# Moving the small tiles of a memory-attention mixer from the working pool to the constants' pool

## The chip, the cores and the metric

The kernel runs on one NeuronCore of a Trainium2 chip. The time is the device time of one execution in microseconds (us). The engines are named as the profile names them: PE is TensorE (matrix products, with its weight loads as PEld), DVE is VectorE, ACT is ScalarE, POOL is GpSimd, and SP is SyncE, whose queue issues most of the DMAs. Of a product on TensorE, the operand that streams through the array is called moving, and the 128 x 128 block that is loaded ahead is called stationary.

## The reference

Eight batches, eight heads, 576 positions, head size 64, 32 memory slots; everything is float32, the four mixer weights are float64 in HBM. For each head the softmax of phi over the positions pools k and v into 32 memory rows, q attends to these, and an MLP mixer over tokens and then over channels follows:

```
a = exp(phi - max(phi, axis=2));  a = a / (sum(a, axis=2) + 1e-09)
k_m = einsum('bhsm,bhsd->bhmd', a, k);  v_m = einsum('bhsm,bhsd->bhmd', a, v)
scores = q @ k_m.T / sqrt(64);  attn = softmax(scores)          # over 32 slots
x = (attn @ v_m), heads side by side                            # (8, 576, 512)
u = x + (relu(x.T @ w_tok1) @ w_tok2).T                         # token mixer, 576 -> 256 -> 576
out = u + relu(u @ w_ch1) @ w_ch2                               # channel mixer, 512 -> 1536 -> 512
```

## The kernel before

Every large product is done in three parts: each operand is split into a high half and a low half in TensorE's fp32r format, and high x high, high x low and low x high are summed in PSUM. So each product of the channel mixer is three matrix instructions.

**The channel mixer** takes most of TensorE's time. The 8 x 576 rows are cut into nine chunks of 512. `Chunk.mm_1` (line 141 in the profile) makes one block f of the hidden layer: 12 instructions of 512 columns, whose moving operands are the chunk's `uh` and `ul`, and whose stationary operands are blocks of the weights `c1h` and `c1l`. ACT and DVE turn the result into `hh` and `hl` (lines 114 and 117). `Chunk.second` (line 180) multiplies these into four accumulators: 12 more instructions of 512 columns, moving operands `hh` and `hl`, stationary operands blocks of the `w_ch2` tiles (two blocks f to a tile: c20, c22, c24, c26, c28, c210, of which two pairs lie in the rooms named c26 and c24 and the last two in the rooms st0 and st1). There are 12 blocks f to a chunk. In the last chunk, the hidden blocks f = 8 to 11 are written to two larger tiles, `stayrest` and `staykv`, which take the rooms of the tags `rest` and `kv`; line 180 then reads its moving operands from there, first 12 instructions of 512 columns (f = 8), then 72 of 256 columns (f = 9 to 11, PSUM tiles named `end`).

**The attention and the token mixer** of a quad (four heads of a batch) are placed between those groups: `mm_A` (line 526, moving `w1h`, `w1l`, stationary `nat`, 256 columns, 14 instructions), `mm_R` (line 545, moving `vh`, `vl`, stationary `Ah`, `Al`, 256 columns, 6 instructions) and `mm_u` (line 566, 288 columns, 9 instructions: three with moving `ah`, `al` and stationary `vh`, `vl`, then six with moving `w2h`, `w2l` and stationary `Rh`, `Rl`), besides small products for the pooling and the scores, and transposes against an identity.

**The order of the work.** For batches 0 and 1 and the first chunk, a planner (list of steps with costs and due times, fixed seed) writes the order; later a table of events does, with two events to a block f. Neither of them knows addresses. In the first hundred us the weights are loaded as float64, brought to float32 by ACT and DVE, and split by ACT and POOL.

**Where tiles lie.** Two pools share each partition of SBUF: `wp` (constants and weights) comes first, and `sb` (working tiles) right behind it. A pool gives its tags rooms in the order of their first use, with all buffers of a tag together, and each buffer rounded up to 32 bytes. `wp` begins at byte 640. The tiles with a size that is no multiple of 128 bytes are `mask` (24 bytes, takes 32) in `wp`, and in `sb` the tags `ps` (4 bytes, two buffers of 32), `ms` (24 bytes, one of 32) and `mx` (72 bytes, two of 96). Whatever follows one of them is displaced. The byte addresses modulo 128 in the kernel before are:

| tiles | read by TensorE at | modulo 128 |
|---|---|---|
| `ident` | transposes | 0 |
| `ones`, `w1h`, `w1l`, `w2h`, `w2l`, `c1h`, `c1l`, w_ch2 tiles in `wp` (c20 to c26) | 526, 566 moving; 141, 180 stationary | 32 |
| `phi`, `kv`, `pr`, `q`/`nat`, the five `wide` rooms (`uh`, `ul`), `rest`, w_ch2 tiles in st0, st1 | 141 moving; 180, 526 stationary; 180 moving at the end (`stayrest`, `staykv`) | 96 |
| `vb`, `vh`, `vl`, `qT`, `kb`, `S` | 545 moving; 566 stationary | 0 |
| `aT`, `ah`, `al`, `Ah`, `Al`, `hh`, `hl`, `Rh`, `Rl` | 180, 566 moving; 545, 566 stationary | 64 |

**The start.** POOL makes the constants; ACT's first instruction is an exponential of one column (`warm`), which brings its table in.

Of the kernel before, what the change touches and what calls it, by code (L numbers as in the profile page):

```python
# [10 lines left out]
F32 = mybir.dt.float32  # L11
# [3 lines left out]
AF = mybir.ActivationFunctionType  # L15
# [5 lines left out]
P = 128  # L21
# [7 lines left out]
def kernel(  # L29
# [24 lines left out]
    nc = tc.nc  # L54
# [7 lines left out]
    NB = S // 32  # L62
# [11 lines left out]
    wp = ctx.enter_context(tc.tile_pool(name="wp", bufs=1))  # L74
    sb = ctx.enter_context(tc.tile_pool(name="sb", bufs=1))
# [12 lines left out]
        nc.gpsimd.memset(mask[32 * i : 32 * i + 32, 4 + i % 2 : 5 + i % 2], 1.0)  # L88
    ones = wp.tile([P, P], F32, name="ones")
    nc.gpsimd.memset(ones, 1.0)  # L90
    warm = sb.tile([P, 1], F32, tag="ps", name="warm", bufs=2)
    nc.scalar.activation(out=warm, in_=ones[:, :1], func=AF.Exp, scale=0.0)


    w1h = wp.tile([P, NC, TT], F32R, name="w1h")
# [140 lines left out]
    class Quad:  # L236
# [98 lines left out]
        def sums(s):  # L335

            nc.vector.tensor_tensor(out=s.r, in0=s.r, in1=ident, op=ALU.mult)
            sm = sb.tile([P, 1], F32, tag="ps", name="pc" + s.n, bufs=2)
            nc.vector.tensor_reduce(out=sm, in_=s.r, axis=AX.X, op=ALU.add)
            return sm  # L340

# [12 lines left out]
            return s.spread_kv  # L354

        def scales(s):
            s.ms = sb.tile([P, 6], F32, tag="ms", name="ms" + s.n, bufs=1)
            sm = sb.tile([P, 1], F32, tag="ps", name="ps" + s.n, bufs=2)
            nc.vector.tensor_scalar_add(out=sm, in0=s.sums(), scalar1=1e-9)
            nc.vector.reciprocal(out=sm, in_=sm)  # L360
            nc.vector.tensor_scalar_mul(out=s.ms, in0=mask, scalar1=sm)
            s.per = sm
# [73 lines left out]
            )  # L436

        def S_max(s):
            s.mx = sb.tile([P, NB], F32, tag="mx", name="mx" + s.n, bufs=2)
            nc.vector.tensor_reduce(out=s.mx, in_=s.S, axis=AX.X, op=ALU.max)  # L440

        def S_sub(s):
# [5 lines left out]
            nc.scalar.activation(out=s.S, in_=s.S, func=AF.Exp, scale=SCALE)  # L448

        def S_sum(s):  # L450
            s.sm = sb.tile([P, NB], F32, tag="mx", name="sm" + s.n, bufs=2)
            nc.vector.tensor_reduce(out=s.sm, in_=s.S, axis=AX.X, op=ALU.add)
            nc.vector.tensor_scalar_add(out=s.sm, in0=s.sm, scalar1=1e-9)
            nc.vector.reciprocal(out=s.sm, in_=s.sm)
# [442 lines left out]
    class EarlyQuad(Quad):  # L897
# [26 lines left out]
            nc.tensor.transpose(s.mt[:, :P], s.m, ident)  # L924

        def phi_diag(s):
            mx = sb.tile([P, 1], F32, tag="ps", name="mc" + s.n, bufs=2)
            nc.vector.tensor_reduce(out=mx, in_=s.mt[:, :P], axis=AX.X, op=ALU.max)
            s.dg = sb.tile([P, 4 * M], F32, tag="pr", name="dg" + s.n, bufs=3)
            nc.vector.tensor_scalar_mul(out=s.dg, in0=ident, scalar1=mx)  # L930
# [459 lines left out]
    for hf in range(2):  # L1390
        w = slice(hf * CW // 2, (hf + 1) * CW // 2)
        for a in range(NKK):
            pool, tag, n = banks.pop(0)
            ps = pool.tile([P, CW], F32, tag=tag, name=f"end{hf}{a}", bufs=n)[:, : CW // 2]
# [37 lines left out]
```

## Time and profile before

| what | value |
|---|---|
| time, median of 3 runs | 826.87 us (826.86 to 827.69) |
| the profiled execution, its own time | 826.83 us |
| span of its trace, first to last instruction | 825.0 us |
| mean granted TensorE clock | 0.987 |
| PE busy | 794.6 us, 96% |
| PEld busy | 655.0 us, 79% |
| DVE, ACT, POOL busy | 418.8, 220.1, 136.0 us |
| DMA | 58.34 MB, mean 71 GB/s |

In the timeline each instruction has its start and its length; matrix instructions are pipelined, so one starts before the end of the one before is shown, and what one costs is the distance from its start to the next start. The chain of waits, followed back from the last instruction, joins instructions of one line into pieces with a start, a length and a count; where PE is never idle, length by count is this same distance. The view by windows gives each engine's busy time and number of instructions in a stretch, and can be restricted to one line.

### The profile page before, as it was taken

To read this page: it belongs to the slowest core of one execution; us is meant where nothing else is said; L and a number is where in the kernel's file an instruction comes from. 1 tells how busy PE (TensorE), PEld (TensorE's weight loads), DVE (VectorE), ACT (ScalarE), POOL (GpSimd) and SP (SyncE) were. 2 spreads that over 40 slices of the span, in tenths; PEclk is the share of its full clock that TensorE was granted. 3 is DMA by queue.
4 is the path that set the end of the run, shared out by engine and by line. 5 is a ranking of instruction groups with operands and counts; after the bars stand their busy time and mean duration, and the time that the engine had idled before them with its cause. 6 is when DMAs were issued, how large, how long until landed. Compare 5 with 4: busy or idle time off the path is not lost.

```text
span 825.0 us, 12037 instructions
## 1 busy us (share of the span) xinstructions
PE 794.6 (96%) x4793; PEld 655.0 (79%) x4793; DVE 418.8 (51%) x699; ACT 220.1 (27%) x430; POOL 136.0 (16%) x134
## 2 busy tenths in 40 slices
PE   6788898999999999999999999999999999999997
PEld 5677677878787878787888888888878788888886
DVE  5897977374437453654455444644374413212115
ACT  4575655222222222131212222122223211210110
POOL 2145432300013000210131013101210200202000
PEclk9799999999999999999999999999999999999999
DMA  8989451224122422142123303231224000200202
GB/s 207 249 225 214 104 160 54 42 72 101 38 44 58 95 58 44 58 81 71 31 71 66 87 16 78 54 65 43 44 62 77 1 1 8 44 1 1 51 1 52
DMA packets 135416, 58.34 MB, mean 71 GB/s; under 512 B 83520, under 2 KB 132672, under 8 KB 135360
## 3 DMA queue, kind: packets, MB, share of 16 engines
q1 hardware_dynamic: 134272, 57.04, 30.5%
q10 hardware_dynamic: 1088, 0.52, 0.3%
q8 instruction: 38, 0.62, 0.3%
q14 instruction: 18, 0.15, 0.1%
HBM read 48.10 MB, written 9.44 MB: 70 GB/s over the span
## 4 chain that ended last, share of the span: by engine, by line
PE 85%; DMA 6%; SPq 4%; DVE 4%; issue 1%; ACT 0%; POOL 0%; DVEq 0%
PE cp L141 34%; PE acc L180 34%; PE u L566 8%; DMA rawc<-in_moe_w_ch_dram 5%; PE Ap L526 3%; PE kvp L347 2%; SPq L911 1%; PE Rp L545 1%; PE end L180 1%; PE sp L425 1%; SPq L270 1%; PE np L491 1%; SPq L266 1%; DVE rawc L628 1%; DMA raww<-in_moe_w_tok_dram 0%
## 5 line engine op out<-in xcount | busy, mean ns | idle before, releaser
L180 PE MATMUL acc<-hh,c 128*128 128x512 f32 x832 | 283.0, 401 | 0.0
L117 DVE SCALAR_TENSOR_TENSOR hl<-cp,hh 128x512 fp32r<-128x512 f32 x104 | 71.8, 690 | 227.1 <-ACT hh L114 227.0
L180 PEld LDWEIGHTS acc<-hh,c 128*128 128x128 f32 x832 | 157.7, 190 | 36.1
L141 PE MATMUL cp<-uh,c1h 128*128 128x512 f32 x432 | 172.0, 398 | 0.0
L141 PE MATMUL cp<-uh,c1l 128*128 128x512 f32 x432 | 169.9, 393 | 0.0
L141 PE MATMUL cp<-ul,c1h 128*128 128x512 f32 x432 | 169.0, 391 | 0.0
L180 PE MATMUL acc<-hl,c 128*128 128x512 f32 x416 | 165.2, 397 | 2.1 <-DVE hl L117 2.1
L114 ACT ACTIVATE hh<-cp 128x512 fp32r<-128x512 f32 x104 | 62.0, 596 | 215.5 <-PE cp L141 215.3
L141 PEld LDWEIGHTS cp<-uh,c1h 128*128 128x128 f32 x432 | 81.1, 188 | 24.3 <-issue 8.6
L141 PEld LDWEIGHTS cp<-uh,c1l 128*128 128x128 f32 x432 | 81.2, 188 | 17.7
L141 PEld LDWEIGHTS cp<-ul,c1h 128*128 128x128 f32 x432 | 81.1, 188 | 16.2
L180 PEld LDWEIGHTS acc<-hl,c 128*128 128x128 f32 x416 | 79.0, 190 | 18.4 <-DVE hl L117 2.5
L192 POOL TENSOR_TENSOR o<-uh,ul 128x512 f32<-128x512 f32 x36 | 46.1, 1307 | 114.9 <-issue 70.2
L471 POOL TENSOR_TENSOR al<-aT,ah 128x576 fp32r<-128x576 f32 x16 | 23.1, 1446 | 250.8 <-ACT ah L467 213.0
L579 ACT COPY rest<-u 128x288 f32<-128x288 f32 (+8 forms) x48 | 15.3, 320 | 95.4 <-PE u L566 90.4
L566 PE MATMUL u<-w2h,Rh 128*128 128x288 f32 x128 | 37.9, 296 | 0.0
L566 PE MATMUL u<-w2h,Rl 128*128 128x288 f32 x128 | 37.8, 296 | 0.0
L566 PE MATMUL u<-w2l,Rh 128*128 128x288 f32 x128 | 37.8, 295 | 0.0
L300 DVE TENSOR_REDUCE pr<-phi 128x128 f32<-128x640 f32 x27 | 35.1, 1303 | 4.9 <-DMA phi<-in_phi_dram 4.6
L587 DVE TENSOR_TENSOR ul<-u,uh 128x288 fp32r<-128x288 f32 (+8 forms) x48 | 16.8, 356 | 33.1 <-ACT uh L581 33.1
L333 POOL PARTITION_ALL_REDUCE psr<-pr x11 | 11.8, 1077 | 111.3 <-DVE pr L300 111.3
L117 DVE SCALAR_TENSOR_TENSOR Rl<-Rp,Rh 128x512 fp32r<-128x512 f32 x16 | 11.1, 691 | 36.6 <-ACT Rh L114 36.5
(148 smaller groups left out, 994.1 us busy)
## 6 DMA issues: line engine op xcount, KB each, us to landing
out_dram<-rows SPq DMA_DIRECT2D x32, 256.0 KB, 4.8
kv<-in_k_dram SPq DMA_DIRECT2D x15, 512.0 KB, 4.3
kv<-in_v_dram SPq DMA_DIRECT2D x15, 512.0 KB, 5.3
q<-in_q_dram SPq DMA_DIRECT2D x192, 36.0 KB, 2.1
rawc<-in_moe_w_ch_dram SPq DMA_DIRECT2D x48, 128.0 KB, 6.1
rawc<-in_moe_w_ch_dram SPq DMA_DIRECT2D x12, 512.0 KB, 7.9
phi<-in_phi_dram SPq DMA_DIRECT2D x16, 256.0 KB, 3.1
q<-in_q_dram SPq DMA_DIRECT2D x16, 128.0 KB, 4.9
```

The costliest lines, as they stand in the source:

```text
L114: nc.scalar.activation(out=h, in_=ps, func=AF.Relu)
L117: nc.vector.scalar_tensor_tensor(out=l, in0=ps, scalar=0.0, in1=f32(h), op0=ALU.max, op1=ALU.subtract)
L141: nc.tensor.matmul(ps, l[:, a, w], r[:, a], start=a == 0 and x == 0, stop=a == NKK - 1 and x == 2,)
L180: nc.tensor.matmul(ps, l_[f // 2][:, f % 2, a * P : (a + 1) * P], r[:, w], start=f == start and x == 0, stop=f == end - 1 and x == 2,)
L192: nc.gpsimd.tensor_tensor(out=s.o[:, a], in0=f32(s.uh[:, a]), in1=f32(s.ul[:, a]), op=ALU.add)
L300: nc.vector.tensor_reduce(out=m.rearrange("p (i m) -> p i m", i=4), in_=s.pt.rearrange("p i j m -> p i m j"), axis=AX.X, op=op,)
L347: nc.tensor.matmul(s.kvp[32 * i : 32 * i + 32, : 2 * D], s.pt[:n, i, j, :], s.kv[i][:n, :, j, :], start=j == 0, stop=j == NC - 1,)
L471: nc.gpsimd.tensor_tensor(out=s.al, in0=s.aT, in1=f32(s.ah), op=ALU.subtract)
L526: nc.tensor.matmul(ps[:, :TT], a, w, start=x == 0, stop=x == len(mm) - 1)
L566: nc.tensor.matmul(ps[:, :HALF], a, r, start=x == 0, stop=x == len(mm) - 1)
L579: nc.scalar.copy(out=rest[0][:, kk, o : o + HALF - n], in_=ps[:, n:HALF])
L587: nc.vector.tensor_tensor(out=ch.ul[:, kk, to], in0=ps[:, :n], in1=f32(ch.uh[:, kk, to]), op=ALU.subtract)
```

## The change

The three small tags move from `sb` to `wp`, ahead of the weights: first `mx` (2 x 96 bytes), then `ms` (32), then `ps` (2 x 32), 288 bytes in all. The first tile of `mx` and that of `ms` are made there and set to zero by two more memsets on POOL, and `warm` reads the zeros of `ms` in place of a column of `ones` scaled by zero. No other instruction is added, removed or put elsewhere.

By the rule above, `w1h` and all that follows in `wp` lies 288 bytes later (modulo 128: 64 in place of 32); `phi` to `rest` in `sb` lie 224 bytes later (64 in place of 96); `vb` to `S` 192 bytes later (64 in place of 0); and `aT` and what follows stays where it is (64). `ident` (0) and `ones` (32) stay too.

```diff
     ones = wp.tile([P, P], F32, name="ones")
     nc.gpsimd.memset(ones, 1.0)
-    warm = sb.tile([P, 1], F32, tag="ps", name="warm", bufs=2)
-    nc.scalar.activation(out=warm, in_=ones[:, :1], func=AF.Exp, scale=0.0)
+
+    small = [
+        wp.tile([P, n], F32, tag=tag, name="small" + tag, bufs=bufs)
+        for tag, n, bufs in (("mx", NB, 2), ("ms", 6, 1))
+    ]
+    for t in small:
+        nc.gpsimd.memset(t, 0.0)
+    warm = wp.tile([P, 1], F32, tag="ps", name="warm", bufs=2)
+    nc.scalar.activation(out=warm, in_=small[1][:, :1], func=AF.Exp)
...
-            sm = sb.tile([P, 1], F32, tag="ps", name="pc" + s.n, bufs=2)
+            sm = wp.tile([P, 1], F32, tag="ps", name="pc" + s.n, bufs=2)
...
-            s.ms = sb.tile([P, 6], F32, tag="ms", name="ms" + s.n, bufs=1)
-            sm = sb.tile([P, 1], F32, tag="ps", name="ps" + s.n, bufs=2)
+            s.ms = wp.tile([P, 6], F32, tag="ms", name="ms" + s.n, bufs=1)
+            sm = wp.tile([P, 1], F32, tag="ps", name="ps" + s.n, bufs=2)
...
-            s.mx = sb.tile([P, NB], F32, tag="mx", name="mx" + s.n, bufs=2)
+            s.mx = wp.tile([P, NB], F32, tag="mx", name="mx" + s.n, bufs=2)
...
-            s.sm = sb.tile([P, NB], F32, tag="mx", name="sm" + s.n, bufs=2)
+            s.sm = wp.tile([P, NB], F32, tag="mx", name="sm" + s.n, bufs=2)
...
-            mx = sb.tile([P, 1], F32, tag="ps", name="mc" + s.n, bufs=2)
+            mx = wp.tile([P, 1], F32, tag="ps", name="mc" + s.n, bufs=2)
```

## The prediction

> **What bounds the kernel now.** I read the page first: engine shares, the slices, the shares of the chain.
>
> ```profile
> span 825.0 us, 12037 instructions
> PE 794.6 (96%) x4793; PEld 655.0 (79%) x4793; DVE 418.8 (51%) x699; ACT 220.1 (27%) x430; POOL 136.0 (16%) x134
> ...
> PEclk9799999999999999999999999999999999999999
> ...
> PE cp L141 34%; PE acc L180 34%; PE u L566 8%; DMA rawc<-in_moe_w_ch_dram 5%; PE Ap L526 3%; PE kvp L347 2%; SPq L911 1%; PE Rp L545 1%; PE end L180 1%; PE sp L425 1%; SPq L270 1%; PE np L491 1%; SPq L266 1%; DVE rawc L628 1%; DMA raww<-in_moe_w_tok_dram 0%
> ```
>
> The reader is to see that the path is TensorE's own stream of products, lines 141 and 180 above all, at nearly full clock. The view by windows says from where on that holds without a gap:
>
> ```profile
> 100.00:140.00 40.00, 36.71 (x264) 29.83 (x263) 31.05 (x44) 20.54 (x37) 14.76 (x10) 0.99 0.39 109
> ...
> 260.00:700.00 440.00, 440.00 (x2600) 363.28 (x2599) 215.39 (x378) 98.71 (x213) 57.41 (x56) 1.00 0.24 52
> ```
>
> (Length, then busy us and count of PE, PEld, DVE, ACT, POOL, then clock, DMA share, GB/s.) In the long stage PE is busy 440 of 440 us, DVE 215. No wait is left there for an edit to remove: only the distance between two starts on PE can change, and it multiplies by the count. Before that the chain of waits has loads and DVE up to about 97 us, then products of PE with DVE's work between them:
>
> ```profile
> 78.60 5.53 DMA rawc<-in_moe_w_ch_dram
> ...
> 94.50 2.35 DVE rawc L628
> ...
> 97.99 4.13 PE acc L180 x12
> ```
>
> The view by windows restricted to one line gives the counts, for line 141 from 97 to 140 us and from 140 to 811, for line 180 the same two, then for lines 566, 526 and 545 from 140 to 811:
>
> ```profile
> 97.00:140.00 43.00, 11.91 (x48) 8.72 (x48) 0.96 0.37 101
> 140.00:811.00 671.00, 287.88 (x1176) 217.29 (x1176) 1.00 0.22 48
> ...
> 97.00:140.00 43.00, 15.10 (x55) 11.28 (x56) 0.96 0.37 101
> 140.00:811.00 671.00, 287.87 (x1166) 213.91 (x1165) 1.00 0.22 48
> ...
> 140.00:811.00 671.00, 70.22 (x468) 67.59 (x468) 1.00 0.22 48
> ...
> 140.00:811.00 671.00, 23.12 (x182) 22.93 (x182) 1.00 0.22 48
> ...
> 140.00:811.00 671.00, 11.70 (x78) 11.03 (x78) 1.00 0.22 48
> ```
>
> **What the distances are now.** The chain, in pieces of one line (start, length, count):
>
> ```profile
> 102.34 1.61 PE Ap L526 x14
> ...
> 405.86 0.71 PE Rp L545 x6
> 406.57 2.74 PE cp L141 x12
> 409.32 1.19 PE u L566 x9
> 410.51 2.80 PE acc L180 x12
> ...
> 796.57 2.79 PE acc L180 x12
> 799.36 8.24 PE cp L141 x36
> 807.60 2.74 PE acc L180 x12
> 810.34 8.64 PE end L180 x72
> ```
>
> Line 141 (moving at 96 modulo 128, stationary at 32) costs 8.24 / 36 = 228.9 ns. Line 180 (moving at 64) costs 2.80 / 12 = 233.3 ns where the stationary tile lies at 96 (the piece at 410.51, block 9) and 2.79 / 12 = 232.5 ns where it lies at 32 (796.57, block 7); I take 232.9. Both lines have the same number of rows and columns, the same order of high and low halves, the same clock. The decisive piece is at 807.60: line 180 again, block 8 of the last chunk, but with its moving operands in `stayrest` and `staykv`, at 96, and its stationary tile at 96 too. It takes 2.74, not 2.79 to 2.80. Seen singly, it even settles lower after its first instructions:
>
> ```profile
> 808.59 0.61 PE L180 MATMUL acc<-stayrest,c 128*128 128x512 f32 x2
> 809.04 0.39 PE L180 MATMUL acc<-staykv,c 128*128 128x512 f32 x1
> 809.27 0.61 PE L180 MATMUL acc<-stayrest,c 128*128 128x512 f32 x2
> 809.72 0.39 PE L180 MATMUL acc<-staykv,c 128*128 128x512 f32 x1
> 809.95 0.39 PE L180 MATMUL acc<-stayrest,c 128*128 128x512 f32 x1
> 810.18 0.28 PE L180 MATMUL end<-stayrest,c 128*128 128x256 f32 x1
> ```
>
> From 808.59 to 810.18 seven instructions start: 1.59 / 7 = 227.1 ns. That is the only place in the kernel where moving and stationary tiles have one remainder, and it is the cheapest for 512 columns. The piece of line 141 just before it, in the same quiet tail, still costs 228.9. So the addresses set some of the distance, and I read it as: equal remainders are best, a difference of 64 costs about 2 ns more, one of 32 about 6. One row argues for less: with 256 columns, the products of `end` (both at 96) cost 8.64 / 72 = 120.0 ns, those of line 526 (32 against 96) only 1.61 / 14 = 115.0. So for short products equality is no gain; it may be a loss.
>
> **The change part by part.**
>
> Line 141, 1176 products in the saturated stage: from 228.9 to 227.1, 1.8 x 1176 = 2.1 us less. Ends: nothing gained if only the average of the whole equal group counts (2.74 / 12 = 228.3, 0.7 us), and 4.0 x 1176 = 4.7 us lost if it is the moving remainder of 64 that is dear (below).
>
> Line 180, of whose 1166 products here all but some 20 at the end are of the slow kind (I take 1150): 232.9 to 227.1, 5.8 x 1150 = 6.7 us less; by the group's average 4.6 x 1150 = 5.3.
>
> Line 566, 288 columns: now 1.19 / 9 = 132.2 ns. Between the two equal prices, 120.0 at 256 columns and 227.1 at 512, a column costs 107.1 / 256 = 0.418 ns, so 288 columns come to 133.4: 1.2 x 468 = 0.6 us more. Line 526: 115.0 to 120.0, 5.0 x 182 = 0.9 more. Line 545: 0.71 / 6 = 118.3 to 120.0, 0.1 more. These three could as well stay, as only the `end` products bear on them; I keep the dear value, because it is the only measured equal pair at 256. The `end` group itself goes from equal at 96 to equal at 64: nothing.
>
> From 97 to 140 us lines 141 and 180 have 48 and 55 products, 0.1 + 0.3 us at the same prices; about half of this stretch is PE's own path: 0.2 less. Before 97 us the cover is the loads, so nothing is counted. The transposes read `ident`, which stays at 0, beside tiles that move; 16 attention quads with some five each, of unknown sign, at 6 ns either way 0.5 us; I count nothing and keep it for the range.
>
> The two new memsets and the other start:
>
> ```profile
> 1.47 0.10 POOL L85 MEMSET mask<- 128x6 f32 x1
> ...
> 2.29 0.21 POOL L90 MEMSET ones<- 128x128 f32 x1
> 2.53 0.20 ACT L92 ACTIVATE warm<-ones 128x1 f32<-128x1 f32 x1 [0.53 <-POOL ones L90]
> 2.56 0.34 POOL L243 MEMSET phi<- 64x128 f32 x2
> ...
> 4.55 2.37 DVE L300 TENSOR_REDUCE pr<-phi 128x128 f32<-128x640 f32 x2 [4.55 <-DMA phi<-in_phi_dram]
> ```
>
> Two at 0.10 us each push POOL's next work, the memsets of `phi`, to end at 3.1 in place of 2.9. DVE's reduction behind them begins at 4.55, and what it waits for is the load. So 1.5 us of cover, cost nothing; without that cover it would be 0.2 us. `warm` starts 0.2 later, with nothing queued behind it on ACT that is due before the reduction has run. The first real users of `ms` and `mx` come many us after the memsets and wait for nothing new. No queue is passed by a step: SP's list of loads is the same.
>
> The loads land at other bytes too, and no row shows a load to the new remainders. The chain gives them 5% of 825 us, 41 us. If a 1024-byte packet took one 32-byte piece more or fewer, that is an estimate of 3% by size, 1.3 us either way; nothing in the trace favours a sign, so I count nothing and put it into the range.
>
> Sum: -2.1 - 6.7 + 0.6 + 0.9 + 0.1 - 0.2 = -7.4 us. Against the profiled execution's own 826.83 us (1.8 more than its span of 825.0, and the same as the median of the runs, 826.87, to 0.04): **819.4 us**.
>
> A rule speaks against any gain. The row to weigh it against is the piece at 807.60, line 180 at 2.74 with its tail at 227.1 ns, where its other pieces have 2.79 and 2.80, and the only thing that I find different is the address. The Trainium skill ("TensorE: Matmul & The Clock Gate", section "Step-by-step: what each phase is for") says that TensorE reads the moving operand and the weights through two independent ports, so that loading the next weights takes nothing from the running product; and its page "SBUF — State Buffer", section "Specifications (TRN2)", gives 16-byte lines, of which 32, 64 and 96 are all multiples. By these two, the sum would be 0 and the time 826.8. The trace, with 227.1 against 232.9 ns on one line, does not agree with that, though it rests on one group.
>
> **The rivals.**
>
> *The moving remainder of 64 is itself the dear thing (slower).* All of line 180's slow products move at 64, whether the stationary tile is at 32 or 96; the cheap ones of lines 141 and 180 move at 96. The change puts every moving operand at 64. Then line 141 rises to 232.9: 4.0 x 1176 = 4.7 us, the quick group at 807.60 loses its 12 x 5.8 = 0.1 and the last 72 as much again, and 97 to 140 adds 0.1: 831.8 us. It decides as soon as line 141's twelve take 2.79 in place of 2.75. Against it speak the products of line 566:
>
> ```profile
> 413.14 0.29 PE L566 MATMUL u<-ah,vh 128*128 128x288 f32 x1
> ...
> 413.53 0.30 PE L566 MATMUL u<-w2h,Rh 128*128 128x288 f32 x1
> ...
> 414.33 0.39 PE L141 MATMUL cp<-uh,c1h 128*128 128x512 f32 x1
> ```
>
> The first three move at 64 and cost 0.39 / 3 = 130 ns, the next six move at 32 and cost 0.80 / 6 = 133. Moving at 64 is not dear there; the three have a difference of 64 and the six one of 32, as my reading wants.
>
> *More comes off than the tail shows.* Equality at 64 may be better than at 96. The best pair of the trace is line 526, 5 ns under `end` at 256 columns. If that came off all products on top of the gain: 5 x 1176 + 5 x 1150 = 11.6, line 566 loses 3.8 x 468 = 1.8 in place of gaining 0.6, and line 526 and 545 stay: about 15 us more, 804.
>
> *Nothing changes.* The distances follow something else than remainders (higher address bits, or the tail's quiet), and 807.60 is chance: then every distance stays and the time is 826.8. (The independent ports of the Trainium skill's page on TensorE, above, would be the reason.) Against it: line 141 directly ahead, equally quiet, is not quicker than in mid-kernel (2.74 at 406.57, 8.24 / 3 = 2.75 here).
>
> **How the numbers follow.** The forecast, 0.60, with its own range of 816 (line 526, 545 and 566 do not rise, and loads or transposes help a little) to 823 (the group's average counts). More comes off, 0.14, 804. Nothing, 0.10, 826.8. Slower, 0.16, 831.8. The range should reach the slow case and half of the way to the case of more, as that one has no sharp price: 809 to 832. 0.2% of this time, 1.7 us, is about what can be told from no change; so faster 0.74, same 0.10, slower 0.16.
>
> **What would show it.** In the changed kernel's chain, pieces of twelve of line 141 at 2.73 and of line 180 at 2.73 (both now 2.75 and 2.80), with no difference between the two lines; line 526 at 1.68 for 14 and line 566 at 1.20 for 9; the start up to 97 us unmoved to half a us; the counts the same. The forecast is wrong if line 141 goes up to 2.79 (rival one), if the two lines stay apart at their old values (no change), if both go to 2.68 or less (more comes off), or if the first 100 us move by over 1.5 us, which would be the loads.

## The result and the profile after

The changed kernel takes 822.08 us (median of 6 runs, 820.20 to 823.43), the kernel before 826.87 (6 runs, 825.77 to 827.69): a ratio of 0.9942, 95% interval 0.9925 to 0.9959. Two later timings of the unaltered change gave 0.9928 (0.9903 to 0.9953) and 0.9926 (0.9899 to 0.9953). So the change is faster by 0.6 to 0.7%, the way that was forecast, with about two thirds of the forecast size (4.8 us of 7.4). The means of the two later timings, each beside runs of the kernel before on the same chip, lie 5.9 and 6.3 us lower.

Between executions of one program the granted TensorE clock differs a little, and the time with it: of 18 runs of the change the quickest, 817.27 us, had 0.995 and the longest, 824.17, had 0.983. The first six runs of the change lie at the lower end (0.982 to 0.989, median 0.983). An estimate that allows for this, a straight-line fit of the time to the clock over these 18 runs and the 47 runs of the kernel before beside the experiments, puts the change 6.0 us below the kernel before (95%: 5.5 to 6.6).

All line numbers after the constants are 7 higher: 148 stands for 141, 187 for 180, 533 for 526, 552 for 545, 573 for 566. The page of the profiled execution (823.43 us, the longest of its six):

```profile
span 821.6 us, 12039 instructions
...
PE 791.2 (96%) x4793; PEld 658.3 (80%) x4793; DVE 420.2 (51%) x699; ACT 219.5 (27%) x430; POOL 135.8 (17%) x136
...
PE cp L148 35%; PE acc L187 34%; PE u L573 8%; PE Ap L533 3%; PE kvp L354 2%; DMA rawc<-in_moe_w_ch_dram 2%; PE Rp L552 1%; DMA phi<-in_phi_dram 1%; PE end L187 1%; DVE rawc L635 1%; SPq L918 1%; PE sp L432 1%; DMA raww<-in_moe_w_tok_dram 1%; PE np L498 1%; SPq L277 1%
```

The reader is to see the same work, two POOL instructions more (the memsets), and the same bound. The chain's pieces at the end of the changed kernel:

```profile
790.67 2.72 PE cp L148 x12
793.39 2.72 PE acc L187 x12
796.11 8.16 PE cp L148 x36
804.27 2.72 PE acc L187 x12
806.99 8.64 PE end L187 x72
```

Both channel products now take 2.72 for twelve, 226.7 ns each (8.16 / 36), where they took 228.9 and 232.9; the group at 804.27, which was the odd one before, is like all others; the last 72 are unmoved at 8.64. In mid-kernel, where the attention's products stand between the groups, less came off:

```profile
402.16 1.67 PE Ap L533 x14
...
406.58 0.71 PE Rp L552 x6
407.30 2.75 PE cp L148 x12
410.04 1.18 PE u L573 x9
411.22 2.75 PE acc L187 x12
```

Line 187 went from 2.80 to 2.75, line 148 stayed where 141 had been (2.74), the 14 products of line 533 rose from 1.61 to 1.67, lines 552 and 573 kept their times. To split the span, take a landmark, the twelve of line 141 that starts at 143.13 us in the kernel before, and the same piece after, from the two chains:

```profile
143.13 2.80 PE cp L141 x12
```

```profile
145.72 2.75 PE cp L148 x12
```

From there to the end the kernel before takes 825.0 - 143.1 = 681.9 us, the changed one 821.6 - 145.7 = 675.9: 6.0 us less. Ahead of it this execution of the change lost 2.6 us; the granted clock from 100 to 140 us was 0.99 before and is 0.92 here:

```profile
100.00:140.00 40.00, 37.42 (x255) 30.80 (x253) 31.37 (x44) 20.38 (x36) 14.95 (x10) 0.92 0.34 96
```

### The profile page after: what moved, and what is told of

Read it like the earlier page. It is cut to its first block, busy times and chain, and to the rows that moved or that the text cites. A ratio compares the mean times of both kernels' runs of the same rounds, so it can differ in the third digit from the quotient of the medians.

```text
span 821.6 us, 12039 instructions
## 1 busy us (share of the span) xinstructions
PE 791.2 (96%) x4793; PEld 658.3 (80%) x4793; DVE 420.2 (51%) x699; ACT 219.5 (27%) x430; POOL 135.8 (17%) x136
## 4 chain that ended last, share of the span: by engine, by line
PE 87%; DMA 4%; DVE 4%; SPq 3%; issue 1%; ACT 0%; POOL 0%; DVEq 0%; ACTq 0%
PE cp L148 35%; PE acc L187 34%; PE u L573 8%; PE Ap L533 3%; PE kvp L354 2%; DMA rawc<-in_moe_w_ch_dram 2%; PE Rp L552 1%; DMA phi<-in_phi_dram 1%; PE end L187 1%; DVE rawc L635 1%; SPq L918 1%; PE sp L432 1%; DMA raww<-in_moe_w_tok_dram 1%; PE np L498 1%; SPq L277 1%
## 5 line engine op out<-in xcount | busy, mean ns | idle before, releaser
L187 PE MATMUL acc<-hh,c 128*128 128x512 f32 x832 | 279.3, 397 | 0.0
L533 PE MATMUL Ap<-w1h,nat 128*128 128x256 f32 x144 | 29.6, 298 | 2.0 <-DVE nat L1020 2.0
```

The lines of the kernel that those rows point to most:

```text
L187: nc.tensor.matmul(ps, l_[f // 2][:, f % 2, a * P : (a + 1) * P], r[:, w], start=f == start and x == 0, stop=f == end - 1 and x == 2,)
L533: nc.tensor.matmul(ps[:, :TT], a, w, start=x == 0, stop=x == len(mm) - 1)
```

## The experiments

The theory: the distance between two products depends on the difference, modulo 128, between where the moving and where the stationary tile lie. The rivals were that the moving remainder alone counts, that a start inside a stretch of 64 or 128 bytes counts, that equality modulo 64 would do, and, for the first stretch, that the loads care where they land. All kernels do the whole computation in the same order of instructions; only the rooms differ. "Rest" is the time from the landmark to the end, as above; GB/s is what the DMA engines moved in the first 60 us.

| kernel | weights / working tiles, modulo 256 | median us | ratio to before, 95% interval | landmark | rest | GB/s |
|---|---|---|---|---|---|---|
| before | 160 / 224, 0, 192 | 826.87 | 1 | 143.1 | 681.9 | 225 |
| the change | 192 / 192 | 822.08 | 0.9942 (0.9925 to 0.9959) | 145.7 | 675.9 | 225 |
| change_again | 192 / 192 | 821.03 | 0.9928 (0.9903 to 0.9953) | 142.8 | 675.8 | 221 |
| change_third | 192 / 192 | 819.96 | 0.9926 (0.9899 to 0.9953) | 146.8 | 675.6 | 226 |
| weights_32_off | 224 / 192 | 829.35 | 1.0033 (1.0015 to 1.0052) | 144.1 | 685.1 | 230 |
| weights_64_off | 128 / 192 | 823.34 | 0.9946 (0.9927 to 0.9964) | 144.4 | 678.3 | 233 |
| all_at_96 | 224 / 224 | 821.16 | 0.9932 (0.9908 to 0.9957) | 144.0 | 676.3 | 217 |
| all_at_128 | 128 / 128 | 820.79 | 0.9929 (0.9906 to 0.9953) | 143.1 | 675.8 | 223 |
| all_at_0 | 0 / 0 | 819.21 | 0.9904 (0.9884 to 0.9925) | 143.0 | 675.4 | 249 |
| all_at_0_again | 0 / 0 | 818.24 | 0.9900 (0.9878 to 0.9922) | 141.1 | 675.3 | 247 |
| all_at_0_third | 0 / 0 | 819.55 | 0.9918 (0.9895 to 0.9941) | 143.8 | 675.4 | 238 |
| weights_32_loads_0 | 160 / 0 | 827.56 | 1.0013 (0.9998 to 1.0028) | 139.9 | 684.9 | 242 |
| token_weights_64_off | 192, token mixer's 128 / 192 | 820.27 | 0.9910 (0.9887 to 0.9934) | 143.1 | 675.2 | 226 |
| zero_token_64 | 0, token mixer's 192 / 0 | 819.04 | 0.9904 (0.9882 to 0.9927) | 143.3 | 674.9 | 238 |

**weights_32_off.** Only `ps` goes to the constants; against the change no working tile moves, only the weights, by 32 bytes.

```diff
-        wp.tile([P, n], F32, tag=tag, name="small" + tag, bufs=bufs)
+        sb.tile([P, n], F32, tag=tag, name="small" + tag, bufs=bufs)
...
-            s.ms = wp.tile([P, 6], F32, tag="ms", name="ms" + s.n, bufs=1)
+            s.ms = sb.tile([P, 6], F32, tag="ms", name="ms" + s.n, bufs=1)
```

(and `mx` in the same way)

> Of the three small tags only ps goes to the constants; mx and ms stay first in the working pool. All working tiles lie where the change puts them (64 modulo 128), the weights in the constants' pool lie at 96, the w_ch2 tiles of blocks 8 to 11 (working pool) at 64. Theory, the difference between the moving and the stationary remainder counts: pieces of twelve of the first channel product take 2.79 to 2.80 us in every block, those of the second 2.79 to 2.80 in blocks 0 to 7 and 2.72 to 2.75 in blocks 8 to 11; against the change about 4.0 ns x 1176 = 4.7 us and 2/3 x 4.4 x 1176 = 3.5 us more, so about 830 us, slower than the kernel before. Rival, only the moving remainder counts: every moving tile lies as in the changed kernel, so all pieces keep 2.72 and the time stays at 822 us.

Measured: 829.35 us; the chain of this kernel near its end:

```profile
797.79 2.80 PE cp L148 x12
800.59 2.80 PE acc L187 x12
803.39 8.40 PE cp L148 x36
811.79 2.72 PE acc L187 x12
```

Moving tiles exactly where the change has them, and yet 2.80 for twelve in place of 2.72, except for the group at 811.79 (block 8), whose stationary tile stayed at the moving tiles' remainder. The rest took 9.2 us more than the change (forecast 8.2) and the kernel is slower than before. The moving remainder alone is out as a cause.

**weights_64_off.** `mx` and `ms` in the constants, `ps` first in the working pool: the weights move by 64 against the change.

```diff
-    warm = wp.tile([P, 1], F32, tag="ps", name="warm", bufs=2)
+    warm = sb.tile([P, 1], F32, tag="ps", name="warm", bufs=2)
```

(and the other tiles of `ps`)

> mx and ms go to the constants, ps stays first in the working pool: working tiles at 64 as in the change, weights in the constants' pool at 0. Theory, a difference of 64 costs about 2 ns more than none with 512 columns and 5 ns less with 256: pieces of twelve of both channel products 2.74 to 2.75 us (the second in blocks 0 to 7 only, 2.72 in blocks 8 to 11), the 14 products of the token mixer's first step 1.61 instead of about 1.67; 1.3 ns x 1176 + 2/3 x 1.6 x 1176 - 0.8 us = about 2 us more than the change, 824 us. Rival, equality modulo 64 is enough: 2.72 everywhere and 822 us or less. Rival, only the moving remainder counts: 2.72 and 822.

Measured: 823.34 us, rest 2.4 us longer than the change's. Its chain:

```profile
401.40 1.60 PE Ap L533 x14
...
794.33 2.75 PE acc L187 x12
797.08 8.24 PE cp L148 x36
805.32 2.72 PE acc L187 x12
```

A difference of 64 costs 228.9 ns (8.24 / 36), as line 141 paid before, now in line 187 as well; with 256 columns it saves (1.60 for 14, not 1.67). So equality modulo 64 isn't enough for long products.

**all_at_0, all_at_96, all_at_128.** Equal as in the change, at other places. The small tags that would displace the rest go to a pool behind the working tiles; for all_at_0:

```diff
+    last_pool = ctx.enter_context(tc.tile_pool(name="last_pool", bufs=1))
...
-        wp.tile([P, n], F32, tag=tag, name="small" + tag, bufs=bufs)
-        for tag, n, bufs in (("mx", NB, 2), ("ms", 6, 1))
+        pool.tile([P, n], F32, tag=tag, name="small" + tag, bufs=bufs)
+        for pool, tag, n, bufs in ((last_pool, "mx", NB, 2), (wp, "ms", 6, 1))
```

(`mx` there throughout; all_at_96 sends `ms` there too, all_at_128 `ps` alone)

> ms and ps go to the constants, mx to a pool of its own behind the working tiles: all tiles that the change puts at 64 modulo 128 lie at 0, so they are equal as well, and no product starts in the middle of a 128-byte stretch. Theory, only equality counts: pieces of twelve 2.72 us, 72 last products 8.64, time as the change, 822 us, within 0.3%. Rival, the 32 cycles or so by which 512 columns take longer than 512 cycles come from a start inside such a stretch: pieces of twelve at 2.56 to 2.64, 72 last at 7.7 to 8.2, time 791 to 806 us.

> Everything that the change puts at 64 lies at 96 modulo 128, mx and ms in a pool behind the working tiles; the loads' rooms in the working pool are then where the kernel before has them. Theory, only equality counts: pieces of twelve at 2.72 us in both channel products, the stage behind the first 145 us takes 674 to 675 us, median within 1.5 us of the change's. Rival, the amount depends on where the equal tiles lie (the start inside a stretch of 64 or 128 bytes): 2.74 or more, or 2.70 or less. Rival, the loads dislike 64: the first stretch is as in the kernel before, 1 to 2 us shorter than in the change.

Measured, in the chain of all_at_0 near its end:

```profile
787.79 2.72 PE cp L149 x12
790.51 2.72 PE acc L188 x12
793.24 8.16 PE cp L149 x36
801.39 2.72 PE acc L188 x12
804.12 8.64 PE end L188 x72
```

and in that of all_at_96:

```profile
792.01 2.72 PE acc L188 x12
794.73 8.16 PE cp L149 x36
```

The amounts agree with the change's to the last digit, and the rests lie between 675.3 and 676.3. Where the equal tiles lie doesn't matter to TensorE; the rival of a start inside a stretch, which would have given 791 to 806 us, is out. The weights of all_at_96 lie where weights_32_off has them; only the working tiles differ, and 36 products take 8.16 us against 8.40. So the stationary remainder alone is out as well: it is the pair that counts. All the equal pairs of long products here are equal modulo 256 too, and none differs by exactly 128, so that 128 is enough is not shown directly. For it speaks that a difference of 96 modulo 256 (weights_32_loads_0, rest 684.9) costs what one of 32 does (weights_32_off, 685.1).

The median of all_at_0 is 2.9 us below the change's first one, its rest only 0.5 us. In its first 60 us it moved data at a higher rate. The rows by windows, of all_at_0, of the change and of change_again:

```profile
0.00:60.00 60.00, 47.18 (x395) 39.83 (x396) 48.86 (x78) 34.69 (x62) 17.16 (x32) 0.89 0.96 249
```

```profile
0.00:60.00 60.00, 43.96 (x382) 37.00 (x383) 45.91 (x75) 32.08 (x60) 14.34 (x31) 0.86 0.94 225
```

```profile
0.00:60.00 60.00, 45.33 (x396) 38.45 (x397) 47.66 (x78) 34.32 (x62) 18.90 (x32) 0.91 0.91 221
```

The rate is higher than in both (249 against 225 and 221 GB/s), but at a clock of 0.91 the unaltered change had as many products done by 60 us (396) as all_at_0 (395).

**The first stretch: change_again, all_at_0_again, all_at_128, weights_32_loads_0, change_third, all_at_0_third.** The two repeats are the same programs. In weights_32_loads_0 `ms` and `ps` stand first in the working pool and `mx` behind it, so that the working tiles lie at 0 and the weights at 32 (modulo 128).

> The changed kernel once more, unaltered, beside the others on one chip. Its profile of before showed the stretch up to about 146 us 2.6 us longer than in the kernel before. Theory, that stretch varies from run to run: here it ends within 1 us of the kernel before's (144 to 145 us), the stage behind it takes 675 us again, and the median is about 820.5 us. Rival, the loads land more slowly at 64 modulo 128: it is over 2 us longer again, 822 to 823 us.

> Everything that the change puts at 64 lies at 0 modulo 128, once more, beside the change on one chip. Theory, only equality counts and the first stretch varies by chance: saturated stage 674.4 us as in the change, median within 1.5 us of the change's. Rival, loads that land at a multiple of 128 are quicker: DMA at 250 GB/s or more from 20 to 60 us, where the others have 210 to 250, the first stretch 1 to 2 us shorter than in the change, the median 1.5 to 3 us below the change's.

> All the equal tiles lie at 128 modulo 256 (0 modulo 128): mx and ms among the constants, ps in a pool behind the working tiles. Theory for TensorE, equality alone: saturated stage 674.4 us, pieces of twelve 2.72. For the loads, where all at 0 (which is 0 modulo 256 too) had landed 14.3 to 15.0 MB by 60 us and the others 13.1 to 14.0: if it is multiples of 128 that suit them, 14.3 MB or more and a median of 818 to 819.5 us; if multiples of 256, 13.1 to 14.0 MB and 821 to 822; if chance, anything between.

> The loads' rooms and all working tiles at 0 modulo 256, the weights in the constants' pool at 32: the loads as with all at 0, the products as with the weights 32 off. If loads and products are two separate effects: saturated stage 683 to 684.5 us as with the weights 32 off, over 14.3 MB landed by 60 us, the first stretch 1 to 2 us shorter, median about 827 us (829.4 less 2). If the early gain of all at 0 was not the loads but the products: 13.1 to 14.0 MB, median 829 or more.

> The changed kernel a third time, for its first stretch and for comparison on this chip: 820.5 to 822.5 us, 13.1 to 14.0 MB landed by 60 us, saturated stage 674.8 us.

> All at 0 modulo 256 a third time: 818 to 819.5 us, 2 to 3 us below the change on the same chip, 14.3 MB or more landed by 60 us, saturated stage 674.4 us. If the difference was chance, within 1 us of the change.

Measured: the change's landmark came at 145.7, 142.8 and 146.8 us in three profiles, the kernel before's at 143.1. That spread of 4 us within one program is why the 2.6 us of the first profile are not put down to the change. It goes with the granted clock: from 100 to 140 us 0.92, 0.95 and 0.91 in the three, and 0.86, 0.91 and 0.86 in the first 60 us. The rate of the loads is another matter: all five profiles (of three programs) in which the rooms in the working pool begin at multiples of 256 have 238 to 249 GB/s, all nine others (of seven programs) 217 to 233, all_at_128 among them with the row

```profile
0.00:60.00 60.00, 45.34 (x394) 38.36 (x395) 47.75 (x78) 34.80 (x62) 17.33 (x32) 0.91 0.90 223
```

So the loads are quicker into multiples of 256, not of 128 (for which all_at_128 is the only profile), and neither the kernel before nor the change has them. weights_32_loads_0 separates the two effects: its rest is that of weights_32_off (684.9 against 685.1), its rate that of the loads at 0. The Trainium skill ("DMA: Bandwidth & Descriptors", section "How a descriptor splits into AXI transactions") says that a transaction must start at a 256-byte boundary, and that a descriptor which doesn't start on one begins at the boundary below and fetches bytes that go unused. It says so of the bytes that are fetched; these runs vary where the bytes land, which that section doesn't speak of, so why the rate differs stays open.

What that is worth in the whole time is less sure. The landmark comes at 139.9 to 143.8 (mean 142.2) in the five, at 142.8 to 146.8 (mean 144.1) in the nine. The three medians at 0 are 819.2, 818.2 and 819.6 us, the change's 822.1, 821.0 and 820.0; on the two chips that ran both, each pair's intervals overlap. The third pair, which was to be 2 to 3 us apart if the gain was real and within 1 us if it was chance, came out 0.4 us apart. The clock is mixed up in all of this: the change's 18 runs have a mean of 0.986, the 18 at 0 one of 0.988. With the same kind of fit to the clock, an estimate, 0.9 us are left (95%: 0.3 to 1.6), of which about 0.4 is the shorter rest. Whether quicker loads bring the better clock about, these runs don't show.

**token_weights_64_off and zero_token_64.** `ps` behind the token mixer's weights, so that these alone are 64 off:

```diff
-    warm = wp.tile([P, 1], F32, tag="ps", name="warm", bufs=2)
-    nc.scalar.activation(out=warm, in_=small[1][:, :1], func=AF.Exp)
...
     w2l = wp.tile([P, NT, S], F32R, name="w2l")
+    warm = wp.tile([P, 1], F32, tag="ps", name="warm", bufs=2)
+    nc.scalar.activation(out=warm, in_=small[1][:, :1], func=AF.Exp)
```

> As the change, but ps is placed behind the token mixer's weights, so that these (moving in lines 526 and 566 of the kernel before) lie at 0 and everything else at 64. Theory, a difference of 64 suits products of 256 columns: the 14 products of the token mixer's first step go from about 1.67 to 1.61 us, those of its third step stay near 1.19 for nine, channel products as in the change (2.72); 196 x 4.5 ns = 0.9 us less than the change, about 821 us. Rival, equality is best at every length: 1.67 or more, and 822 us or more.

> As with all at 0, but the token mixer's weights lie at 64, a difference of 64 from what they are multiplied with. Theory, the short products of the token mixer's first step like that difference: their pieces of 14 take 1.63 to 1.65 us in place of 1.67, 0.3 to 0.9 us less than with all at 0, the best of the versions tried. Rival, no difference: as with all at 0.

Measured, the piece of 14 in the chain of token_weights_64_off:

```profile
399.11 1.65 PE Ap L533 x14
```

It is 1.65, a third of the way back from 1.67 to 1.61, and the rest is 0.4 to 0.7 us shorter than in the change. zero_token_64 has the same:

```profile
399.37 1.65 PE Ap L534 x14
```

The direction held, the size of the first expectation didn't. In weights_64_off the same tiles have the same difference and take 1.60; the two kernels differ in that the groups around these products have a difference of 64 there too, and why that matters wasn't tried. zero_token_64 has the shortest rest (674.9). In time neither can be told apart from its counterpart without the shift: zero_token_64 819.04 us, all_at_0 818.2 to 819.6; token_weights_64_off 820.27, the change 820.0 to 822.1.

## Why the prediction was right, and where its size was off

**What bounds the kernel.** Right: only distances on PE changed, and the stage in which PE is never idle gave all of the gain.

**The decisive piece.** Right, though it stood on one group of twelve. The piece at 807.60 settled at 227.1 ns because both tiles had one remainder: in the change every group far from other products does the same (2.72, 226.7 ns), and weights_32_off takes it away by moving the stationary tiles alone. The order of the three prices was right as well: equal 226.7, 64 apart 228.9, 32 apart 232.5 to 233.3 (2.79 / 12 and 8.40 / 36).

**The terms.** Distances between starts, averaged in the two traces from the landmark on: line 141, 1175 products, 231.6 to 230.3 ns, so 1.5 us less (forecast 2.1); line 180, 1152 products, 235.5 to 231.0, 5.2 less (6.7); line 526, 168 products, 115.2 to 119.5, 0.7 more (0.9); lines 566 and 545 unchanged (forecast 0.6 and 0.1 more). Sum -6.0 where the same terms were forecast at -7.2. The step that was mis-sized is "from 228.9 to 227.1, 1.8 x 1176" and its like for line 180: it gave the settled price to every product. Behind shorter products the gain comes late. Count the places of an unbroken run of long products from its start, the last one ahead of a shorter product left out. Line 141 went from 230.0 to 231.5 ns at places 2 to 5, from 229.0 to 227.9 at 6 to 11, and only from the 12th on from 228.9 to 226.7; line 180 went from 232.7 to 231.6, from 233.2 to 227.5 and from 232.6 to 226.7. So the settled gain was even a little larger than forecast, and the products at the start of a run gave little of it or none. The timeline of the changed kernel, behind a piece of line 533:

```profile
403.67 0.40 PE L187 MATMUL acc<-hh,c 128*128 128x512 f32 x1
403.91 0.40 PE L187 MATMUL acc<-hl,c 128*128 128x512 f32 x1
404.14 0.62 PE L187 MATMUL acc<-hh,c 128*128 128x512 f32 x2
404.60 0.39 PE L187 MATMUL acc<-hl,c 128*128 128x512 f32 x1
404.83 0.62 PE L187 MATMUL acc<-hh,c 128*128 128x512 f32 x2
...
406.19 0.39 PE L187 MATMUL acc<-hh,c 128*128 128x512 f32 x1
406.42 0.28 PE L552 MATMUL Rp<-vh,Ah 128*128 128x256 f32 x1
```

Five products take 404.83 - 403.67 = 1.16 us, 232 ns each; the seven after them 1.59 / 7 = 227.1. That makes a piece of 2.75 us where 2.72 was due. The prediction had seen a slow start in the piece at 807.60 ("settles lower after its first instructions"), took the price behind it, and kept the group's average for the end of its range. There it was gone afterwards (2.72 at 804.27), where the group stands behind long products. Behind short ones it stays with equal remainders all around. What causes it wasn't tried.

**The start.** The two memsets cost nothing that can be seen beside the spread between executions; no run takes them out alone. The forecast of a start "unmoved to half a us", and its sign that a move of over 1.5 us in the first 100 would be the loads, were both too bold. The group of line 180 that starts at 97.99 us before starts at 99.56, 96.61 and 100.41 in the three profiles of the change: the start moves both ways within one program, so that sign can't tell the loads from chance. The change's three medians run from 820.0 to 822.1 us, all a little above the forecast of 819.4.

**The rule that spoke against it.** The Trainium skill's pages "TensorE: Matmul & The Clock Gate", section "Step-by-step: what each phase is for" (two independent read ports), and "SBUF — State Buffer", section "Specifications (TRN2)" (16-byte lines), left no room for an effect. weights_32_off decides it: moving tiles unmoved, weights shifted by 32 bytes, two lines, and 2.80 in place of 2.72. The measurement decides against the rule.

**The rivals.** That a moving remainder of 64 is dear: out, all moving tiles lie there now. That nothing changes: out. That more comes off with equality at a better place: out for TensorE by all_at_0 and all_at_96; what may come off at 0 besides, about 1 us by the estimate above, lies in part ahead of the landmark. The prediction had put the loads at "1.3 us either way" without a sign, and the change doesn't reach the multiples of 256.

## What to carry to other kernels

Where TensorE streams without a gap, compare the distance between starts on lines with the same shapes: an unexplained few per cent can be the tiles' addresses, and one group that happens to be laid out otherwise is a free experiment. Lay moving and stationary tiles at one remainder modulo 256 for long products, and where the loads bound the time, begin the rooms that they fill at multiples of 256; a tile of four bytes ahead of them spoils both. Here the second raised the rate of the loads, and was worth about 1 us of the time, by an estimate. Before a difference of a few us in a first stretch is put down to an edit, compare the granted clock there. A price measured inside a long run holds for the long run only: count the groups that start behind a break apart.

## What the runs showed of the hardware that was not expected

- fp32r products of 512 columns, back to back, each with its own weight load: 226.7 ns with moving and stationary tiles at one remainder modulo 256 (0, 128, 192 or 224 alike), 228.9 at a difference of 64, 232.5 to 233.3 at 32. A difference of exactly 128 was not run.
- With 256 columns the order turns: 120.0 ns (8.64 / 72) equal, 115 (1.61 / 14) at a difference of 64.
- Behind shorter products, long ones take 231.5 ns at places 2 to 5 of their run even with equal remainders, and 226.7 from the 12th on.
- The loads of the first 60 us run at 238 to 249 GB/s into rooms at multiples of 256 bytes, at 217 to 233 into others, multiples of 128 included.
- Executions of one program are granted clocks of 0.982 to 0.995 (18 runs of the change), and take 817.3 to 824.2 us with it.
- Why the distance between products depends on the two addresses together, these runs don't show.
